# Crossbar transposes in layer norm and SwiGLU, and the earlier weight gradient stage

## The chip, the cores and the metric

The kernel runs on one core of a Trainium2 chip. The time is that of one execution on the device, in microseconds (us), as the median of repeated runs. TensorE (PE) multiplies matrices into PSUM, VectorE (DVE) and ScalarE (ACT) work elementwise and copy PSUM out, GpSimd (POOL) does small elementwise work, and SyncE (SP) issues transfers. ScalarE and GpSimd can issue transfers too. All transfers run on the core's 16 DMA engines. The "crossbar" below is the path in those engines that transposes two-byte data on its way.

## What is computed

Forward and backward of a block with layer norm, a segment-recurrent attention with memory, and a SwiGLU gate. There are S = 2048 rows of D = 640, H = 32 heads of 128, F = 1728, 64 segments of 32 rows, each with 8 memory rows. All tensors are bfloat16.

```python
xn = layernorm(x)                                  # rows, no affine part
mem = mem0                                         # 8 rows
for s in range(64):                                # one after the other
    h = concat([mem, xn[32*s:32*s+32]])            # 40 rows
    q, k, v = h @ Wq, h @ Wk, h @ Wv               # 32 heads of 128
    p = softmax(mask(q @ k.T * 128**-0.5))
    o = (p @ v) @ Wo
    mem, out_s = o[:8], o[8:]
z = (silu(xn @ w1) * (xn @ w3)) @ w2
out = x + concat(out_s) * silu(z)
# returned: out, and the gradients of x, mem0, Wq, Wk, Wv, Wo, w1, w3, w2
```

The stages in order are: layer norm; forward SwiGLU; the projections of the first rows; the forward chain over segments; the output stage; the backward chain; the weight gradients (with the part of x's gradient that comes through q, k and v); Wo's gradient; w2's gradient; the backward SwiGLU loop with layer norm's backward; the gradients of w1 and w3.

## The kernel before, where the change touches it

A transpose is made in one of two ways: on TensorE into PSUM, followed by a copy, or by the crossbar.

```python
def turned_load(k, dst, src):
    k.nc.sync.dma_start_transpose(dst, src)

# layer norm: xn is stored twice, as it is and turned
k.dma(k.XN[tt * P:(tt + 1) * P, :], xn[:])
for dc in range(DC):
    nc.tensor.transpose(pt[:, dc, :], xn[:, dc * P:(dc + 1) * P], k.ident[:])
k.copy(xnT[:], pt[:])
k.dma(k.XNT[...], xnT[:])

# forward SwiGLU, 4 blocks of 512 rows, 14 chunks of F (the last has 64 rows)
nc.gpsimd.dma_start(Wv[:], ...); k.x_rows(k.HRO, k.XN, nc.gpsimd)   # Wk follows at block 1
nc.scalar.dma_start(xnT[:], k.XNT[...])
for fc in range(FC):
    ...                                    # 5 matmuls into pg, 5 into pu, 128x512 each
    sig = sigmoid(pg); sl = pg * sig; ut = copy(pu); hBT[fc] = sl * ut
    ds = ...                               # three VectorE operations
    nc.sync.dma_start(k.SLT[...], sl); nc.sync.dma_start(k.DUT[...], ds)   # sl, ds: 2 buffers
for ti in range(BLK // P):
    ...                                    # 28 matmuls 128x320 into pz; gb, dz, gs; stores on nc.sync
    # 5 transposes of gs, copied, stored as GST; 14 transposes of hBT, copied in halves, stored as HB

# weight gradients: 8 groups of four heads (qd), 22 tiles of 120 rows (96 x rows, then 24 memory rows)
NF = NTL - 2; NB = 5; order = [NF, NF + 1] + list(range(NF))
def dturn(u):                              # dS turned by the crossbar
    turned_load(k, dST[:], st["l", u][0][:].rearrange("p j c -> p (j c)"))
def s2(u):                                 # gradients of v, k, q for one tile
    for i in range(3):                     # lhs = (P, dS, dST)
        ...                                # 4 matmuls into r6p (2 PSUM banks), copied to gr
        # the two last tiles are spilled to GSP and fill partitions 120 to 127 of gr
def s3(u):                                 # x rows only: 12 transposes 96x96 into t6g, copied to a ring
def s4(u):                                 # each full 128 x rows: 2 x 12 matmuls 128x320, added to acc
def wg(qd, i):                             # 20 tiles x 5 matmuls 128x512
for p in range(NTL):
    s2(u + 3); ld_to(u + 3 + NB); dturn(u + 4); s3(u + 2); s4(u)     # with bounds

# Wo's gradient: rows of OR on nc.sync, two buffers; hb loaded from HB on nc.scalar along the way
# w2's gradient: per row tile, 5 transposes of gz into one PSUM buffer, copied into gzT,
# which lies in one tile with w1T and w3T (crossbar loads); then 448 matmuls 128x320 (w2a)
# backward SwiGLU, 8 blocks of 256 rows
pg = ...                                   # 5 matmuls 128x256 per chunk; ggT = pg * du, guT = pg * sl
pgx = ...                                  # 56 matmuls 128x320 per row tile; PSUM: psC bufs=2, psD bufs=1
for (gT, dst) in ((ggT, ggtok), (guT, gut)):
    ...                                    # 14 transposes, copied by VectorE and ScalarE
nc.sync.dma_start(GU[rows, :], gut[:])
# w1, w3: 320 matmuls 128x432 with ggtok, then 320 with gutok_all, loaded from GU
```

Of the kernel before, what the change touches and what calls it, by code (L numbers as in the profile page):

```python
# [40 lines left out]
class K:  # L41
# [76 lines left out]
    def build_masks(self, pool, scr):  # L118
        nc = self.nc
        GE = ALU.is_ge  # L120
        n, nx = 120, 96
# [7 lines left out]
        for (c0, w) in ((nx, 8), (0, 32)):  # L129
            v1 = a1[:, c0:c0 + 3 * w].rearrange("p (s c) -> p s c", c=w)  # L130
            v2 = a2[:, c0:c0 + 3 * w].rearrange("p (s c) -> p s c", c=w)
            sel(v1, 1, -nx, [[-8, 3], [0, w]])
            sel(v1, -1, nx + 7, [[8, 3], [0, w]])
            sel(v2, 1, 0, [[-32, 3], [0 if w == 8 else -1, w]])
            sel(v2, -1, 31, [[32, 3], [0, w]])
# [8 lines left out]
        sel(b1[:], 1, -32, [[0, 40]])  # L144
        sel(b2[:, 0:32], 1, 0, [[-1, 32]])
# [6 lines left out]
    def setup_dram(self):  # L152
# [7 lines left out]
        self.XNT = mk("XNT", (D, S))  # L160
        self.SLT = mk("SLT", (F, S))
        self.DUT = mk("DUT", (F, S))
        self.HB = mk("HB", (S, F))
# [3 lines left out]
        self.GST = mk("GST", (D, S))  # L167

        self.NR = S + 8 * T
        self.GXA = mk("GXA", (S, D))  # L170
# [23 lines left out]
        for tl in range(self.NTL):  # L194
            n = self.geo(tl)[3]
            self.PR.append(mk(f"PR{tl}", (n, H, P)))
            self.DSR.append(mk(f"DSR{tl}", (n, H, P)))
# [3 lines left out]
        self.GSP = mk("GSP", (8, 3, 160, 512))  # L201
# [26 lines left out]
    def m_src(self, tl, w, c0, c1):  # L228
# [3 lines left out]
        r0 = self.geo(tl)[2]  # L232
        while t < end:
            e = min(end, t - t % 4 + 4)
            XS = self.store(w)[t // 4, g, 0:8, t % 4:t % 4 + e - t]
            for i in range(2 if w == "qv" else 1):
                X = XS[:, :, i] if w == "qv" else XS
                out.append((r0 + 8 * (t - 3 * tl), r0 + 8 * (e - 3 * tl), X[:, :, c0 - 1024 * g:c1 - 1024 * g].rearrange("r t c -> t r c"), i))
# [8 lines left out]
    def m_rows(self, A, t):  # L247
        r = 120 * (t // 3) + self.geo(t // 3)[2] + 8 * (t % 3)
        return A[r:r + 8, :]

    def x_rows(self, A, X, eng):
        n = self.NTL - 1
        eng.dma_start(A[0:120 * n, :].rearrange("(t r) d -> t r d", r=120)[:, 0:96],
                      X[0:96 * n, :].rearrange("(t r) d -> t r d", r=96))
        eng.dma_start(A[120 * n:120 * n + 32, :], X[96 * n:self.S, :])


# [102 lines left out]
def phase3_Afwd(k, W4, Wv, Wk_):  # L360
# [5 lines left out]
    with tc.tile_pool(name="b0", bufs=1) as io, tc.tile_pool(name="b0s", bufs=3) as stp, \  # L366
            tc.tile_pool(name="b0p", bufs=4, space=bass.MemoryType.PSUM) as ps:
        xs = io.tile([P, DC, k.NB0], BF16, name="b0x")
        nc.sync.dma_start(xs[:], k.XNT[:, 0:k.NB0].rearrange("(dc p) t -> p dc t", p=P))
# [21 lines left out]
    with tc.tile_pool(name="ast", bufs=1) as st, tc.tile_pool(name="achain", bufs=1) as ch, \  # L391
# [22 lines left out]
        def ride_ld(t):  # L414
            x0 = k.NB0 + 24 * t
            b, sub = t // 4, t % 4
            if sub == 0 and x0 < S:
                w = min(96, S - x0)
                rt = ch.tile([P, DC, 96], BF16, name="ride", tag="ride")
                nc.sync.dma_start(rt[:, :, 0:w], k.XNT[:, x0:x0 + w].rearrange("(dc p) s -> p dc s", p=P))  # L420
# [145 lines left out]
        def ld(w, tl, qd, eng=nc.sync):  # L566
# [4 lines left out]
            k.load_x(r, 0, k.x_src(tl, w, c0, c0 + 512), eng)  # L571
# [11 lines left out]
        def scores(tl, qd):  # L583
# [8 lines left out]
            for j in range(4):  # L592
                kv = kT[:, h0 + j, 0:n].rearrange("p (s c) -> p s c", c=40)
                nc.tensor.matmul(sp[:, j, nx:n], qT[:, j, :], kv[:, :, 0:8], start=False, stop=True,
                                 skip_group_check=True)
                nc.tensor.matmul(sp[:, j, 0:nx], qT[:, j, :], kv[:, :, 8:40], start=False, stop=True,
# [19 lines left out]
        def norm(tl, qd, eng=nc.gpsimd, q=nc.gpsimd):  # L616
# [6 lines left out]
            q.dma_start(k.PR[tl][:, h0:h0 + 4, :], Pb[0:n])  # L623
# [19 lines left out]
        def pv(tl, qd, q=nc.gpsimd):  # L643
# [3 lines left out]
            if 4 * tl < k.NO:  # L647
                pt = ps.tile([P, 4, 96], F32, name="xot", tag="x", bufs=5)
                for j in range(4):
                    nc.tensor.matmul(pt[:, j, :], v[0:n, j * P:(j + 1) * P], PTs[qd % 2][0:n, j, 0:96], start=True, stop=True)  # L650
# [110 lines left out]
def gx_ld(k, xs, x0, eng):  # L761
    w = min(P, k.S - x0)
    eng.dma_start(xs[:, :, 0:w], k.GST[:, x0:x0 + w].rearrange("(dc p) t -> p dc t", p=P))
# [13 lines left out]
def phase3b_out(k, Wo, W0, W4):  # L777
# [12 lines left out]
    with tc.tile_pool(name="oio", bufs=1) as io, tc.tile_pool(name="oac", bufs=1, space=bass.MemoryType.PSUM) as pa, \  # L790
# [6 lines left out]
        def ld(b, qd):  # L797
# [3 lines left out]
            if nt == 3:  # L801
                src = k.OR[120 * tl:120 * tl + 360, c0:c0 + 512].rearrange("(t r) c -> r t c", r=120)[0:96]
            else:
                src = k.OR[120 * tl:120 * tl + nx, c0:c0 + 512].rearrange("(t r) c -> r t c", t=1)
# [45 lines left out]
        def gox_ld(x0):  # L850
            xs = io.tile([P, DC, P], BF16, name="g0x", tag="g0x", bufs=2)
            gx_ld(k, xs, x0, nc.scalar)
# [34 lines left out]
        while g0:  # L887
# [6 lines left out]
    later = [(k.GWO[0:120 * n, :].rearrange("(t r) d -> t r d", r=120)[:, 0:96], k.GS[0:96 * n, :].rearrange("(t r) d -> t r d", r=96)),  # L894
             (k.GWO[120 * n:120 * n + 32, :], k.GS[96 * n:k.S, :])]

    for s in range(3):
# [3 lines left out]
        for b in range(2):  # L901
            dst = k.HRO[120 * tl0:120 * tl0 + 120 * (n - 1), :].rearrange("(t r) d -> t r d", r=120)[:, 96 + 8 * s:104 + 8 * s]
# [3 lines left out]
            later.append((k.m_rows(k.HRO, t1 + 1)[:, cols], k.FS[t1, 32 * b:32 * b + 8, :]))  # L906
# [998 lines left out]
```

## Time and profile before

| | before |
|---|---|
| median of 3 runs | 5610.01 us (5604.01 to 5610.44) |
| span of the profiled execution | 5608.7 us |
| granted TensorE clock, mean | 0.936 |
| TensorE matmul busy | 4787.0 us (85%) |
| TensorE weight loads busy | 3029.7 us (54%) |
| VectorE, ScalarE, GpSimd busy | 2245.6, 1758.4, 1562.8 us |
| moved by DMA | 845.92 MB in 1,100,096 packets, 602,753 of them under 512 B |
| forward chain (521 to 1841 us) | 1320 us, TensorE busy 1166.05 |
| output stage (1898 to 2020 us) | 122 us, DMA share 1.02 |
| backward chain (2147 to 3415 us) | 1268 us, TensorE busy 1163.37 |
| w1 and w3 gradients (5485 to 5609 us) | 124 us, TensorE busy 118.64 |

The busy time of an engine is the sum of its instructions. A group of instructions is one line of the kernel with one operation and shape; its idle time is what the engine stood still just before such instructions, with the releaser that came last. The clock is the share of full speed that TensorE was granted. The DMA share is the mean busy share of the 16 engines.

### The profile page before, as it was taken

What the parts mean: (1) busy time and instruction counts of PE and PEld (TensorE: products, weight loads), DVE (VectorE), ACT (ScalarE), POOL (GpSimd) and SP (SyncE); (2) the same over time, 40 slices, a digit from 0 to 9 for tenths busy, and PEclk for the clock granted to TensorE, in tenths of its full rate; (3) what the DMA queues carried; (4) which work ended last, traced back from release to release, by engine and by line L of the source; (5) the groups of instructions that cost most, each with busy time, mean ns of one, the idle gap of its engine ahead of it and who ended that gap; (6) DMA issues with size and microseconds to landing.
All of it is one profiled execution on the core that took longest, in us unless ns stands there. A gap on an engine that the chain in (4) does not pass through costs nothing. (4 is left out here: it accounts for less than half of the span.)

```text
span 5608.7 us, 161247 instructions
## 1 busy us (share of the span) xinstructions
PE 4787.0 (85%) x64913; PEld 3029.7 (54%) x65308; DVE 2245.6 (40%) x7110; ACT 1758.4 (31%) x4913; POOL 1562.8 (28%) x2675
## 2 busy tenths in 40 slices
PE   4987888888898767989899995978888888799999
PEld 2554555555555434656565663555455545566665
DVE  5833555555555323445454441232122212211451
ACT  2422555555555322323333321222122212200111
POOL 0000334434443122333333333234223423210000
PEclk9998999999999778999999997999999999899999
DMA  7553455555544696667666657576547655657332
GB/s 248 171 184 89 137 160 157 159 157 157 159 151 138 155 175 160 182 182 194 180 183 174 183 160 135 109 145 130 108 103 140 134 104 114 139 178 187 104 117 91
DMA packets 1100096, 845.92 MB, mean 151 GB/s; under 512 B 602753, under 2 KB 988077, under 8 KB 1096673
## 3 DMA queue, kind: packets, MB, share of 16 engines
q1 hardware_dynamic: 854523, 582.31, 40.0%
q0 software_dynamic: 95696, 155.10, 10.9%
q10 hardware_dynamic: 149130, 98.17, 6.4%
q8 instruction: 515, 8.44, 0.7%
q14 instruction: 232, 1.90, 0.1%
HBM read 476.95 MB, written 303.09 MB: 139 GB/s over the span
## 5 line engine op out<-in xcount | busy, mean ns | idle before, releaser
L1410 PE MATMUL wg<-gr,hr 128*128 128x512 bf16 x2352 | 532.6, 386 | 16.5 <-DVE grs L1353 7.6
L1389 PE MATMUL g<-w,ghacc 128*128 128x320 bf16 x3072 | 471.8, 314 | 0.0
L1410 PEld LDWEIGHTS <-hr 128*128 128x128 bf16 x2400 | 237.9, 99 | 305.0 <-issue 35.8
L1389 PEld LDWEIGHTS <-ghacc 128*128 128x128 bf16 x3072 | 309.8, 103 | 129.9
L308 PEld LDWEIGHTS <-hx 128*32 128x32 bf16 x7680 | 179.2, 97 | 168.0 <-issue 10.2
L1344 PE MATMUL r6p<-r,dST 120*128 120x128 bf16 (+1 forms) x704 | 74.7, 234 | 224.6 <-DMA dST<-dS 121.3
L90 DVE CAST wgo<-wg 128x512 bf16<-128x512 f32 x72 | 47.5, 688 | 539.0 <-PE wg L1410 289.5
L90 DVE CAST stg<-bank 128x512 bf16<-128x512 f32 x256 | 177.1, 692 | 206.5 <-PE bank L308 204.1
L327 PEld LDWEIGHTS <-gkv 128*8 128x8 bf16 x8192 | 190.5, 87 | 107.9 <-DVE gkv L1002 24.9
L611 ACT ACTIVATE xP<-xsp,xnm 120x120 bf16<-120x120 f32 (+1 forms) x704 | 240.5, 376 | 10.6 <-DVE xnm L607 5.2
L245 POOL DMA_DIRECT2D r<-GOS x256 | 144.0, 565 | 291.8 <-PE r6p L1344 221.8
L660 POOL DMA_DIRECT2D OR<-xv x163 | 93.0, 570 | 472.2 <-ACT xv L659 350.0
L1154 POOL DMA_DIRECT2D DSR<-gdS x176 | 101.5, 576 | 428.0 <-DVE gdS L1152 403.6
L92 ACT CAST wgo<-wg 128x512 bf16<-128x512 f32 x48 | 25.8, 589 | 595.8 <-PE wg L1410 595.8
L622 POOL TENSOR_TENSOR xP<-xP,xrz 120x480 bf16<-120x480 bf16 x163 | 161.9, 993 | 136.2 <-ACT xP L611 96.2
L1398 DVE TENSOR_TENSOR ghacc<-ghacc,g 128x320 f32<-128x320 f32 x192 | 93.7, 488 | 251.0 <-PE g L1389 251.0
L1344 PEld LDWEIGHTS <-dST 120*128 120x128 bf16 (+1 forms) x704 | 55.0, 103 | 247.4 <-DMA dST<-dS 151.1
L1351 ACT CAST gr<-r6p 120x512 bf16<-120x512 f32 x160 | 94.0, 588 | 295.1 <-PE r6p L1344 294.9
L1152 DVE SCALAR_TENSOR_TENSOR gdS<-gdp,Dx,gPr 120x120 bf16<-120x120 f32 (+1 forms) x680 | 182.9, 331 | 0.0
L1223 PE MATMUL gbank<-WqT,ident 128*128 128x512 bf16 x453 | 161.0, 405 | 20.7 <-issue 13.1
L308 PE MATMUL gbank<-WoT,gox 128*32 128x512 bf16 x2560 | 154.2, 387 | 25.2 <-POOL gox L957 21.9
L327 PE MATMUL bank<-Wo,oTm 128*32 128x320 bf16 x4032 | 171.9, 323 | 0.1
(339 smaller groups left out, 10933.5 us busy)
## 6 DMA issues: line engine op xcount, KB each, us to landing
QVS<-stg SPq DMA_DIRECT2D x128, 256.0 KB
gqv<-QVS SPq DMA_DIRECT2D x108, 192.0 KB
vTt<-VTD SPq DMA_DIRECT2D x64, 320.0 KB
VTD<-gvT POOLq DMA_DIRECT2D x168, 120.0 KB, 3.6
DSR<-gdS POOLq DMA_DIRECT2D x168, 120.0 KB, 3.6
dS<-DSR SPq DMA_DIRECT2D x168, 120.0 KB
P<-PR SPq DMA_DIRECT2D x168, 120.0 KB
gPr<-PR SPq DMA_DIRECT2D x164, 120.0 KB
```

The source lines that it names most:

```text
L90: return nc.vector.tensor_copy(out, in_)
L245: eng.dma_start(d, src if src.shape[0] > 1 else src[0])
L308: k.nc.tensor.matmul(bank[32 * g:32 * g + 32, :], x[:, dc, :], W[:, dc, c0:c0 + 512], start=(dc == 0), stop=(dc == k.DC - 1), tile_positio ...
L327: k.nc.tensor.matmul(pm[p0:p0 + nq, 0:320], x[:, h, :], W[:, h, 320 * b:320 * b + 320], start=(first and i == 0), stop=(last and i == 15), ...
L611: nc.scalar.activation(Pb[0:n, j, 0:n], sp[0:n, j, :], ACT.Exp, bias=nmx[0:n, j:j + 1], scale=k.scale, accum_out=Z[0:n, j:j + 1])
L622: eng.tensor_tensor(Pb[0:n, :, 0:n], Pb[0:n, :, 0:n], bc_last(rz[0:n], n), ALU.mult)
L1152: nc.vector.scalar_tensor_tensor(dS[0:n, j, 0:n], dp[0:n, j, :], Dx[0:n, j:j + 1], Pr[0:n, j, 0:n], op0=ALU.subtract, op1=ALU.mult)
L1154: nc.gpsimd.dma_start(k.DSR[tl][:, h0:h0 + 4, :], dS[0:n])
L1223: nc.tensor.matmul((bA if g in ("W1", "G1", "G2") else bB)[:], k.ident[:], WqT[:, 0, 0:512], start=True, stop=True)
L1344: nc.tensor.matmul(pr[:, j * P:(j + 1) * P], lhs[i][0:n, j, :], rw[i][0:n, j * P:(j + 1) * P], start=True, stop=True)
L1389: nc.tensor.matmul(pg[:], ring[:, i, j, r0:r0 + P], Ws[qd][i][:, j, 320 * h:320 * h + 320], start=(i == 0 and j == 0), stop=(i == 2 and j ...
L1410: nc.tensor.matmul(accs[dc][:], hr[:, tl, dc * P:(dc + 1) * P], grs[i][:, tl, :], start=(tl == 0), stop=(tl == NF - 1))
```

## The change

It has two parts. Layer norm and both SwiGLU stages let TensorE turn nothing any more: normalized rows, GS, h, gz and gg are turned by the crossbar, either from DRAM when they are loaded or from SBUF to SBUF, so that PSUM and the copies out of it are spared. As all crossbar transposes are issued by SyncE, the stores and plain loads of these stages go to GpSimd's and ScalarE's queues. In return, the weight gradient stage is the earlier one: it also takes the memory rows through the part that yields x's gradient (20 windows of 128 rows rather than 16), has 22 tiles of 120 rows in the weight products instead of 20 filled to 128, turns dS on TensorE instead of by the crossbar, and has three buffers for its loads instead of five. With it, the memory rows come first in each tile of 120 again, and P and dS are stored with rows of 120 instead of 128.

```diff
 # layer norm
-            for dc in range(DC):
-                nc.tensor.transpose(pt[:, dc, :], xn[:, dc * P:(dc + 1) * P], k.ident[:])
-            xnT = io.tile([P, DC, P], BF16, name="xnT_t", tag="xnT_t")
-            k.copy(xnT[:], pt[:])
-            k.dma(k.XNT[:, tt * P:(tt + 1) * P].rearrange("(dc p) t -> p dc t", p=P), xnT[:])
 # forward SwiGLU
-            nc.scalar.dma_start(xnT[:], k.XNT[:, b0:b0 + BLK].rearrange("(dc p) t -> p dc t", p=P))
+            turned_load(k, xnT[:], k.XN[blk * BLK:(blk + 1) * BLK, :])       # in fetch(), a block ahead
-                nc.sync.dma_start(k.SLT[fc * P:fc * P + fsz, b0:b0 + BLK], sl[:fsz])
-                nc.sync.dma_start(k.DUT[fc * P:fc * P + fsz, b0:b0 + BLK], ds[:fsz])
+                nc.gpsimd.dma_start(k.SLT[fc * P:fc * P + fsz, b0:b0 + BLK], sl[:fsz])
+                nc.gpsimd.dma_start(k.DUT[fc * P:fc * P + fsz, b0:b0 + BLK], ds[:fsz])
-                # transposes of gs and of hBT, their copies, stores of GST and of HB by rows
+            nc.gpsimd.dma_start(k.HB[0:(FC - 1) * P, b0:b0 + BLK].rearrange("(c p) t -> p c t", p=P), hBT[:, 0:FC - 1, :])
 # projections, rides of both chains, GS for the output stage (the same pattern)
-        nc.sync.dma_start(xs[:], k.XNT[:, 0:k.NB0].rearrange("(dc p) t -> p dc t", p=P))
+        turned_load(k, xs[:], k.XN[0:k.NB0, :])
 # weight gradients
-    NF = NTL - 2
-    NB = 5
+        NB = 3
-            dST = io.tile([P, 4, P], BF16, name="dST6", tag="dST6", bufs=4)
-            turned_load(k, dST[:], st["l", u][0][:].rearrange("p j c -> p (j c)"))
+            for j in range(4):
+                nc.tensor.transpose(pt[:, j, :], dS[0:n, j, :], k.ident[0:n, 0:n])
+            nc.vector.tensor_copy(dST[0:n, :, 0:n], pt[0:n])                 # s1(u), two buffers
-            nc.sync.dma_start(dS[0:n], k.DSR[tl][:, h0:h0 + 4, :])
-            nc.sync.dma_start(Pr[0:n], k.PR[tl][:, h0:h0 + 4, :])
+            nc.sync.dma_start(dS[0:n, :, 0:n], k.DSR[tl][:, h0:h0 + 4, :])
+            nc.sync.dma_start(Pr[0:n, :, 0:n], k.PR[tl][:, h0:h0 + 4, :])
+            for tl in range(NTL):
+                u = u0 + tl
+                ld(u + 4)
+                s2(u + 2, 0); s2(u + 2, 1); s1(u + 3); s3(u + 1, 0, 2); s2(u + 2, 2); s3(u + 1, 2, 3)
+                s4(u)                                                        # with bounds
 # Wo's gradient
-                nc.sync.dma_start(orrs[q][:, h * a:h * a + h, :], ...)
+                nc.scalar.dma_start(orrs[q][:, h * a:h * a + h, :], ...)
+        for f in range(0, F, 432):
+            late.append((hb[:, :, f:f + 432], k.HB[f:f + 432, :]))           # turned_load
 # w2's gradient and backward SwiGLU
-                        # 5 transposes of gz, copied
+                        turned_load(k, gzT[:, :, tt * P:(tt + 1) * P], gz[:, tt, :])
-                            # 14 transposes of ggT and 14 of guT, copied; GU stored by rows
+                                turned_load(k, ggtok[:, b0 // P:b0 // P + 2, fc * P:fc * P + fsz], ggT[0:fsz, fc, :])
+                        nc.gpsimd.dma_start(GU[0:FR, cols].rearrange("(c p) t -> p c t", p=P), guT[:, 0:FC - 1, :])
-                        tc.tile_pool(name="c5pc", bufs=2, space=bass.MemoryType.PSUM) as psC, \
-                        tc.tile_pool(name="c5pd", bufs=1, space=bass.MemoryType.PSUM) as psD:
+                        tc.tile_pool(name="c5pc", bufs=4, space=bass.MemoryType.PSUM) as psC, \
+                        tc.tile_pool(name="c5pd", bufs=2, space=bass.MemoryType.PSUM) as psD:
-                    nc.scalar.dma_start(gutok[:, t0:t0 + 2, :], GU[t0 * P:(t0 + 2) * P, :].rearrange("(t p) f -> p t f", p=P))
+                    turned_load(k, gutok[:, :, 432 * f:432 * f + 432], GU[432 * f:432 * f + 432, :])
```

The last load stands in `for f in range(4)`. GXA, which carries x's gradient through q, k and v to the last loop, has 2,560 rows instead of 2,048, and is read there in pieces of 32 to 96 rows.

## The prediction

> **What bounds the kernel now.** I first read the page's slices: TensorE is 80 to 99% busy nearly everywhere, so the time is TensorE's work plus its pauses, and a mean over the kernel says little. So I cut the span into stages and read busy times stage by stage. Columns: stretch, length, then busy us of TensorE, of its weight loads, VectorE, ScalarE, GpSimd, then granted clock, DMA share, GB/s.
>
> ```profile
> 0.00:62.00 62.00, 11.19 (x81) 7.57 (x82) 33.18 (x143) 11.30 (x25) 3.35 (x22) 1.00 0.82 255
> 62.00:330.00 268.00, 226.63 (x1293) 118.32 (x1310) 176.62 (x360) 99.85 (x161) 3.13 (x4) 0.92 0.55 186
> 3415.00:3460.00 45.00, 1.17 (x8) 0.79 (x9) 1.24 (x3) 0.54 (x1) 13.98 (x26) 0.54 0.91 176
> 3460.00:4960.00 1500.00, 1257.50 (x9640) 793.34 (x9687) 360.74 (x711) 356.78 (x576) 491.83 (x886) 0.92 0.60 122
> 4960.00:5137.00 177.00, 175.70 (x1280) 125.87 (x1280) 29.28 (x65) 12.03 (x32) 24.19 (x46) 0.99 0.74 232
> 5137.00:5225.00 88.00, 74.57 (x528) 48.05 (x528) 9.98 (x24) 9.59 (x21) 1.43 (x2) 0.92 0.47 93
> 5225.00:5485.00 260.00, 240.23 (x1904) 164.10 (x1905) 145.53 (x353) 42.78 (x65) 26.67 (x23) 0.99 0.38 117
> ```
>
> These are layer norm, forward SwiGLU, the start of the weight gradients, the weight gradients, the Wo gradient, the w2 gradient and the backward SwiGLU. The two recurrent chains (1,320 and 1,268 us) stand between them and are hardly touched. The weight gradients are the odd stage: 243 us of their 1,500 have no matmul, and the clock is 0.92. The groups and the timeline of that stage say why:
>
> ```profile
> L1344 PE MATMUL r6p<-r,dST 120*128 120x128 bf16 x672 | 71.3, 234 | 221.9 <-DMA dST<-dS 121.3 <-ACT gr L1351 69.0 <-ACT grs L1351 31.4
> ```
> ```profile
> 4043.26 3.42 PE L1389 MATMUL g<-w,ghacc 128*128 128x320 bf16 x24
> 4046.53 0.39 PE L1344 MATMUL r6p<-r,P 120*128 120x128 bf16 x4
> 4046.75 0.39 PE L1344 MATMUL r6p<-r,dS 120*128 120x128 bf16 x4
> 4051.11 0.60 PE L1344 MATMUL r6p<-r,dST 120*128 120x128 bf16 x4 [3.97 <-DMA dST<-dS]
> 4051.51 1.17 PE L1374 MATMUL t6g<-ident,gr 96*128 96x96 bf16 x12
> 4052.48 5.46 PE L1389 MATMUL g<-w,ghacc 128*128 128x320 bf16 x24
> ```
>
> The turned dS comes by crossbar and is late again and again; and after such a pause the same 24 matmuls take 5.46 us instead of 3.42. In an undisturbed unit TensorE still waits 0.45 us for ScalarE's copy before the third r6p group. Two more pauses lie in the chain that ended last (start, length, what):
>
> ```profile
> 5147.94 18.26 DMA x<-in_B_w_dram
> 5230.34 8.31 DMA sl<-SLT
> ```
>
> **What the skill says.** "DMA: Bandwidth & Descriptors", Latency and other measured facts, gives a DMA transpose 261 GB/s when its middle dimension isn't contiguous. The trace disagrees. While the w1 and w3 transposes ran (5140 to 5166 us), the DMA view reads:
>
> ```profile
> q1 hardware_dynamic: 16223, 4.38, 103.4%
> ```
>
> that is 1.034 x 16 engines x 26 us = 430 engine-us for 16,223 packets (4.38 MB), 26.5 ns for one of some 256 B, or about 155 GB/s on 16 engines. I use 26.5 ns. The same page, Specifications, puts the least transfer at full rate at 512 B; the trace agrees in kind: 186 B packets of ScalarE's queue took 15 ns in the forward chain (12 GB/s an engine), 1,054 B packets of SyncE's 54 ns (19.5 GB/s). Its section Queues, rings and completion order says that an engine takes turns between queues but drains one queue in order; the trace of before keeps stores and bulk loads on different queues there, so it doesn't show that case. "TensorE: Matmul & The Clock Gate", Why this matters for your kernels, says that an idle gap over about 3 us puts the array back to half its clock; the 5.46 against 3.42 us above agrees.
>
> **Weight gradients, by unit.** A unit is one 120-row tile for four heads; a group of four heads has 22 units, and there are 8 groups. Costs at full clock from start to start in the timeline: four r6p matmuls 0.22 us, twelve 96-wide transposes 0.51 (so I estimate 0.64 at 120 wide, 0.21 for four), 24 g matmuls 3.26, and 100 wg matmuls 21.75.
> - Before, a group: 22 x (0.67 + 0.51) + 16 x 3.26 + 300 x 0.2175 = 26 + 52 + 65 = 143 us; + 22 x 0.45 for ScalarE + about 8 of bank waits around wg = 161. Measured 1500/8 = 187.5. So some 26 us a group go to late dST and to the slow clock after it.
> - After, the memory rows are back in: 20 windows instead of 16, 22 tiles in wg instead of 20, 120-wide transposes, and four more transposes a unit for dS: 22 x (0.67 + 0.21 + 0.64) + 20 x 3.26 + 330 x 0.2175 = 33 + 65 + 72 = 170 us. The 0.45 us is filled, because dS's transposes and eight others stand between the second and third r6p group. With the same 8 us around wg: 178.
>
> So 27 us of work are added to each group, but the path loses the crossbar wait. 8 x 178 = 1,424 against 1,500: -76. The start (45 us, held by a 3 MB load of hr with small loads queued behind it) no longer needs a dST before its first work: about -10. VectorE gets a 0.40 us copy more per unit (the chain's 120x480 copies take 0.40) and still has some 2.5 us of work in 4.8; ScalarE some 2.2. Packets: the dS and P loads fall to 240 B pieces, 960 of them instead of 240 of 1 KB; at about 20 ns that is 1.2 us of 16 engines a unit instead of 0.75, but 512 transpose packets (0.85 us) go. DMA shouldn't bind. With three buffers instead of five I add 20 us of new waits. Stage: -66.
>
> **Layer norm and forward SwiGLU (0 to 330).** Removed from TensorE: 80 transposes in layer norm, 304 in SwiGLU (17.6 + 7.9 us busy), with ScalarE's and VectorE's copies (25 and 10 us). At full clock the rest is 560 x 0.217 + 448 x 0.136 = 182 us. VectorE's own chain is 56 x 2.63 (0.685 + 0.684 + 0.420 + 0.419 + 0.417) + 16 x 2.61 = 189 us, so VectorE becomes the bound. Before, TensorE's queue holds the layer norm transposes, so the first SwiGLU matmul stands at 61.9 us. Now it needs four normalized tiles and one crossbar load of 2,560 packets (4.2 us, plus issue and landing): about 42 us. Layer norm's 29 us on VectorE then lies partly beside it. Against this: the stores of sl and ds, two buffers each, now share GpSimd's queue with Wv, HRO and Wk (about 13 MB), so some 40 us of the early overlap stall. I put the end at 285 instead of 330: -45. Block 0 of the projections then waits for a 3,360-packet crossbar load (5.6 us) instead of a plain one: +4.
>
> **Output stage and chains.** The output stage has DMA at 1.02; four crossbar loads of GS come on top: +3. Rides by crossbar (14 in each chain, 0.8 us of DMA) and PR stores in 240 B pieces lie beside matmuls: 0.
>
> **Wo gradient and SwiGLU backward.** Wo gradient: hb comes by crossbar, 27,648 packets = 46 us of DMA instead of an estimated 19; 0.74 x 177 + 27 = 158 of 177 us, still hidden: 0. The w2 stage loses its 80 transposes (about 6 us) and the 18.26 us wait, since gzT's copy no longer stands in TensorE's way; 448 x 0.136 = 61 plus a little: 68 instead of 88, -20. In the block loop 448 transposes go: 14 take 1.0 us, so 32 us, and their copies (16 x (0.52 + 0.52) on VectorE, which feeds the accumulators), with twice the PSUM buffers: 560 x 0.114 + 896 x 0.151 = 199 plus load waits, 215 instead of 260: -45. The last stage: four crossbar loads of GU start only when the loop has ended, 46 us of DMA plus about 8 of drain, against 60 us of matmuls ahead of them: just hidden, +3 for risk. Sum -62.
>
> **Sum.** -66 - 45 + 4 + 3 - 62 = -166; 5610 - 166 = about 5,444. I shade it to 5,440.
>
> **Rivals.**
> - The added work shows and the waits stay: dS, P and row loads with three buffers are late as dST was. Then a group costs 170 + 8 + 26 = 204, the stage +132 over before, and the whole 5,640. For it: 60% DMA share already, small packets. Against it: the crossbar needed a load, a wait on SyncE and a transpose in series, the load alone only the first, with about two units (9.5 us) to land.
> - Stores behind bulk loads: the forward stage stalls until Wv, HRO and Wk are in, and gains nothing: about 5,490. For it: Wk took 41.5 us to land before. Against: those loads slowed the same stores before, from the other queue.
> - The crossbar becomes the bound in the backward stage (SyncE issues all transposes; gutok late): that stage gains only 30: about 5,470.
>
> **Range and chances.** The sum rests mostly on the weight gradients, where work and waits move against each other. If both smaller rivals come true in part, 5,520; if no new waits come and the loop runs clean, 5,360. Eight in ten: 5,350 to 5,560. Two per cent is 5,498 and below: 0.72; within 2%: 0.23; slower: 0.05.
>
> **What would show it.** Right: weight gradients near 1,440 to 1,450 us with TensorE busy over 93% and no wait on dS; first forward matmul near 42 us and VectorE over 90% busy after 110; backward loop near 215 with no gap at gutok. Wrong: TensorE waiting for dS, P or rows in the weight gradients; the clock there still 0.92; sl or ds waiting for SLT or DUT past 110 us.

## The result, and the profile after

The changed kernel takes 5,569 us (median of four runs, 5,551 to 5,573) against 5,610: a ratio of 0.992, interval 0.990 to 0.995. It is faster by 41 us where 170 were predicted, and lies outside the predicted 5,350 to 5,560. The same table of stages for the kernel after (columns as in the prediction: stretch, length, busy us of TensorE, its weight loads, VectorE, ScalarE, GpSimd, then granted clock, DMA share, GB/s):

```profile
39.00:300.00 261.00, 197.67 (x996) 96.56 (x1007) 179.79 (x405) 85.49 (x142) 96.83 (x172) 0.91 0.60 205
3409.00:3430.00 21.00, 1.92 (x14) 1.27 (x15) 1.15 (x3) 0.59 (x1) 11.09 (x21) 0.59 1.01 187
3430.00:4923.00 1493.00, 1409.62 (x11396) 915.07 (x11394) 457.14 (x989) 382.21 (x615) 453.80 (x818) 0.97 0.43 103
4923.00:5123.00 200.00, 183.66 (x1280) 128.31 (x1280) 29.26 (x65) 13.15 (x31) 24.01 (x46) 0.94 0.81 205
5123.00:5210.00 87.00, 66.27 (x448) 42.95 (x449) 7.17 (x18) 4.98 (x14) 2.97 (x5) 0.90 0.65 127
5210.00:5448.00 238.00, 211.77 (x1456) 138.55 (x1456) 125.55 (x315) 12.66 (x31) 47.34 (x52) 0.95 0.73 158
```

Side by side, from the same stretches and from the first and last matmul of each stage:

| stage | before | after | moved | predicted |
|---|---|---|---|---|
| start to the first projection matmul | 331.5 | 300.6 | -31 | -41 |
| forward chain (window) | 1,320 | 1,341 | +21 | 0 |
| start of the weight gradients | 45 | 21 | -24 | -10 |
| weight gradients | 1,500 | 1,493 | -7 | -56 |
| Wo gradient | 177 | 200 | +23 | 0 |
| w2 gradient | 88 | 87 | -1 | -20 |
| backward block loop | 260 | 238 | -22 | -45 |
| w1 and w3 gradients | 123 | 122 | -1 | +3 |

The rest (projections -4, prologue of the backward chain +8) is small. Three things stand out. TensorE is busier in the weight gradients (1,410 us instead of 1,258), at 0.97 of its clock instead of 0.92, in the same time: waits were exchanged for work. The Wo gradient, which was to stay hidden, has 16 us without a matmul and a clock of 0.94. And the w2 gradient lost its transposes (66 us busy instead of 75) but no time.

**Weight gradients, inside.** The timeline of TensorE in the middle of a group (start, duration, instruction):

```profile
4007.32 0.39 PE L1343 MATMUL r6p<-r,P 120*128 120x128 bf16 x4
...
4008.83 3.42 PE L1379 MATMUL g<-w,gT 128*128 128x320 bf16 x24
4012.09 0.39 PE L1343 MATMUL r6p<-r,P 120*128 120x128 bf16 x4
```

One unit takes 4.77 us from start to start, without a pause; the prediction's terms give 0.67 + 0.21 + 0.64 + 3.26 = 4.78. So the unit was priced right: 170 us a group, 1,363 in all. The other 130 us lie mostly at the heads of the groups. There the timeline of SyncE's queue (how long it took over each run of transfers) and that of TensorE read:

```profile
3966.66 29.50 SPq L1406 DMA_DIRECT2D out_dram<-wgo  x10
3996.25 0.39 SPq L1314 DMA_DIRECT2D dS<-DSR  x1
```
```profile
3995.85 0.38 PE L1343 MATMUL r6p<-r,P 120*128 120x128 bf16 x4 [1.95 <-DVE wgo L90]
...
3997.69 0.63 PE L1343 MATMUL r6p<-r,P 120*128 120x128 bf16 x4
...
3999.53 0.58 PE L1331 MATMUL t<-ident,dS 120*128 120x120 bf16 x4 [0.77 <-DMA dS<-DSR]
```

The dS of the fourth unit is written behind the ten last stores of wg in SyncE's queue, and these wait for wg to end. So it starts only when TensorE already wants it. Around it a group of four costs 0.58 to 0.63 us instead of 0.39: the granted clock is 1.00 until 3996 us and 0.57 from 3996 to 4004. The slow clock thus begins after the wait of 1.95 us for a copy of wg, ahead of the wait for dS. The groups view adds up the waits:

```profile
L1331 PE MATMUL t<-ident,dS 120*128 120x120 bf16 x700 | 68.9, 224 | 31.7 <-DMA dS<-DSR 28.2 <-DVE wgo L90 2.1 <-DVE gr L1348 0.7
```

Pauses are 1,493 - 1,410 = 83 us in all. 1,363 + 83 leaves 47 us. By the trace's record of the granted clock, 69 us of the matmul time ran at half clock, which costs some 35 us (an estimate: half of 69). The other 12 us are matmul time beyond the sum.

### The profile page after: what moved, and what is told of

The parts are those of the page before. It is cut to its first block, busy times and chain, and to the rows that moved or that the text cites. A ratio compares the mean times of both kernels' runs of the same rounds, so it can differ in the third digit from the quotient of the medians.

```text
span 5570.0 us, 163086 instructions
## 1 busy us (share of the span) xinstructions
PE 4878.7 (88%) x65768; PEld 3095.4 (56%) x66108; DVE 2311.4 (41%) x7334; ACT 1728.7 (31%) x4879; POOL 1685.9 (30%) x2802
## 5 line engine op out<-in xcount | busy, mean ns | idle before, releaser
L1401 PE MATMUL wg<-gr,hr 120*128 120x512 bf16 (+1 forms) x2640 | 587.9, 383 | 17.1 <-DVE dST L1333 13.0
L1379 PE MATMUL g<-w,gT 128*128 128x320 bf16 x3840 | 549.5, 300 | 0.0
L1401 PEld LDWEIGHTS <-hr 120*128 120x128 bf16 (+1 forms) x2640 | 257.8, 99 | 339.2 <-issue 45.4
L1379 PEld LDWEIGHTS <-gT 128*128 128x128 bf16 x3840 | 369.3, 98 | 137.0
L1388 DVE TENSOR_TENSOR ghacc<-ghacc,g 128x320 f32<-128x320 f32 x240 | 117.2, 488 | 276.4 <-PE g L1379 276.4
L1346 ACT CAST gr<-r6p 120x512 bf16<-120x512 f32 (+1 forms) x176 | 103.2, 587 | 362.9 <-PE r6p L1343 338.7
L92 ACT COPY gT<-t6g 128x960 bf16<-128x960 bf16 (+5 forms) x216 | 167.0, 792 | 121.5 <-PE t6g L1362 120.5
L1131 POOL DMA_DIRECT2D VTD<-gvT x176 | 130.7, 744 | 157.5 <-ACT gvT L1130 129.8
L1362 PE MATMUL t6g<-ident,gr 120*128 120x120 bf16 (+1 forms) x2112 | 172.5, 221 | 3.3 <-DVE wgo L90 2.7
```

The source lines that it names most:

```text
L92: return nc.scalar.copy(out, in_)
L1362: nc.tensor.transpose(pt[:, i - i0, j, :], st["g", u, i][0:n, j * P:(j + 1) * P], k.ident[0:n, 0:n])
L1379: nc.tensor.matmul(pg[:], ring[:, i, j, r0:r0 + P], Ws[qd][i][:, j, 320 * h:320 * h + 320], start=(i == 0 and j == 0), stop=(i == 2 and j ...
L1401: nc.tensor.matmul(accs[dc][:], hr[0:n, tl, dc * P:(dc + 1) * P], st["g", NTL * qd + tl, i][0:n, :], start=(tl == 0), stop=(tl == NTL - 1))
```

## Experiments: the weight gradients

**One more buffer for dS, P and rows.**

```diff
-        NB = 3
+        NB = 4
-                for i in range(3):      # loads ahead of wg's stores
+                for i in range(4):
```

> After the change, with four buffers instead of three for dS, P and rows in the weight gradients, so that the first four units of a group are loaded ahead of the stores of wg instead of three. Theory: dS of the fourth unit stands on SyncE's queue behind the stores of wg, so it comes late at the head of every group (28 us in all) and the array restarts at half clock (some 20 us more): the stage falls from 1,493 us to about 1,450, the whole to about 5,525. Rival: the pauses at the heads are accumulators waiting for copies, not loads; then the stage stays above 1,480 and the whole above 5,555.

Measured: 5,553 us, ratio 0.990 (0.988 to 0.992). The stage went from 1,491 to 1,470 us (first r6p of dST to last wg), the wait for dS from 28.2 to 12.8 us, of which 10.7 is the very first group, and the clock from 0.97 to 0.98. So both theories held in part. The queue cost some 21 us, which is more than the spread of this stage: it took 1,491 to 1,501 us in the nine kernels that leave it as it is. Of the 70 us of pauses that remain some 55 are waits for copies of accumulators, most of them around wg, and 53 us of matmul time still run at half clock.

**The kernel before, with dS turned by TensorE, between the second and third r6p group, and nothing else changed.** This separates the crossbar wait, which the change was to remove, from the memory rows, which it put back.

```diff
-            turned_load(k, dST[:], st["l", u][0][:].rearrange("p j c -> p (j c)"))
+            for j in range(4):
+                nc.tensor.transpose(pt[:, j, :], dS[0:n, j, :], k.ident[0:n, 0:n])
+            nc.vector.tensor_copy(dST[0:n, :, 0:n], pt[0:n])
```

> The kernel before, with one thing changed: dS turned by TensorE and VectorE instead of by the crossbar. Theory of the prediction (crossbar waits and half clock cost some 26 us a group): a group then has 22 x (0.67 + 0.21 + 0.51) + 16 x 3.26 + 65 = 148 us of work and, with the pauses that the changed kernel shows around wg (15 us), 163: stage about 1,305 instead of 1,500, whole about 5,415. Rival: the loads of dS and rows are themselves late, or SyncE's queue is blocked by stores as in the changed kernel; then the stage stays above 1,400 and the whole above 5,510.

Measured: 5,496 us, ratio 0.981 (0.977 to 0.985); the stage 1,401 us. It went past the changed kernel, but its stage stopped at the rival's figure, for a reason that neither theory had. TensorE's groups and ScalarE's timeline in that run:

```profile
L1352 PE MATMUL r6p<-r,dST 120*128 120x128 bf16 (+1 forms) x704 | 71.2, 226 | 110.0 <-ACT gr L1359 80.0 <-ACT grs L1359 25.2 <-DMA eo_s<-SR 2.8
```
```profile
4005.88 0.31 ACTq L267 DMA_DIRECT2D r<-GOS  x1
4006.29 0.80 ACT L92 COPY ghacc<-t6g 128x768 bf16<-128x768 bf16 x1 [4.28 <-DMA r<-QVS]
```

ScalarE issues the loads of gO's rows between its copies, in order. Its copy at 4006.29 came 4.28 us late because the load ahead of it could not go out yet, and TensorE waited for the copies behind.

**The same with those loads on SyncE.**

```diff
-                k.load_x(r, 0, src, nc.scalar if nm_ == "g" else nc.sync)
+                k.load_x(r, 0, src, nc.sync)
```

> The kernel before with dS turned by TensorE, as in the run before of that kind (stage 1,401 us), and the rows of gO in the weight gradients issued by SyncE instead of ScalarE. Theory: ScalarE is held up issuing those loads, so its copies of r6p and of the turned rows are late (105 us of TensorE waiting for ScalarE); the stage falls to about 1,310 and the whole to about 5,405. Rival: ScalarE's copies are late for want of buffers or accumulators; then the stage stays above 1,380, whole above 5,475.

Measured: 5,444 us, ratio 0.971 (0.968 to 0.973); the stage 1,357 us. The direction is the theory's, the size about half: 41.5 us of waits for ScalarE remain, 130 of them with at most 0.6 us, the 0.24 us in every unit before the third r6p group among them. The changed kernel has hardly any there (13, with 10.3 us in all), with eight transposes in between; that order is taken over in the last run below.

## Experiments: where the stages behind and ahead lost their gain

**The SwiGLU part alone.** The kernel before with the layer norm, SwiGLU and ride part of the change, but its own weight gradients, row order and 1 KB rows of P.

```diff
-        self.HB = mk("HB", (S, F))
+        self.HB = mk("HB", (F, S))
-                nc.sync.dma_start(rt[:, :, 0:w], k.XNT[:, x0:x0 + w]...)
+                turned_load(k, rt[:, :, 0:w], k.XN[x0:x0 + w, :])
+    # and layer norm, forward SwiGLU, Wo gradient, SwiGLU backward as in the kernel after
```

> The kernel before with only the layer norm and SwiGLU part of the change (crossbar loads, rides by crossbar, stores moved), its own weight gradients, row order and 1 KB rows of P. By the stages of the changed kernel: about -35 to the end of the projections, +8 ahead of the backward chain, +23 Wo gradient, -2 w2, -21 block loop, -2 last: about 5,580 if the forward chain keeps its old length (P stores are the cause of its 21 us), about 5,602 if the rides are.

Measured: 5,596 us, ratio 0.9986 (0.9974 to 0.9999). This half, priced at 100 us, gives almost nothing when alone, and the whole is nearer the figure for slow rides (5,602); the forward chain is taken up below. Its stages are those of the changed kernel: last forward matmul at 285, Wo gradient 195, w2 gradient 85, loop 232.

**GpSimd issues what ScalarE issued in the Wo and w2 gradients.**

```diff
-                nc.scalar.dma_start(orrs[q][...], ...)      # OR's columns
-                    nc.scalar.dma_start(out6f[...], ot[:])  # Wo's gradient
-                            nc.scalar.dma_start(out9[...], ot[...])  # w2's gradient
+    # the same three on nc.gpsimd
```

> After the change, with the stores of Wo's and w2's gradients and the loads of OR's columns put out by GpSimd instead of ScalarE. Theory: ScalarE, which also copies half of the accumulators, stands still while such a transfer waits for its turn behind crossbar loads; freed of them, the Wo gradient falls from 200 us to about 182 and the w2 gradient from 86 to about 71: whole about 5,536. Rival: the crossbar loads fill the DMA engines there (share 1.18) and nothing else can land whoever issues it; then Wo stays at 195 or more and w2 at 83 or more, whole about 5,565.

Measured: 5,553 us, ratio 0.990 (0.987 to 0.992). The w2 gradient fell to 71 us, the Wo gradient rose to 214 (32 us of waiting for OR's columns): the theory held for one and the rival for the other. Freeing ScalarE is not what the Wo gradient lacks.

**h's crossbar loads in twelve pieces; six buffers for sl and du; w2's stores on GpSimd.**

```diff
-        for f in range(0, F, 432):
-            late.append((hb[:, :, f:f + 432], k.HB[f:f + 432, :]))
+        for f in range(0, F, 144):
+            late.append((hb[:, :, f:f + 144], k.HB[f:f + 144, :]))
-                            sl = bp.tile(..., tag="sl5", bufs=3)   # and du5
+                            sl = bp.tile(..., tag="sl5", bufs=6)
```

> After the change, three edits in three stages behind the weight gradients. Wo gradient: h's crossbar loads in twelve pieces over tiles 4 to 11 instead of four pieces over tiles 4 to 7. Theory: the stage lost 23 us because these loads bunch (DMA share 1.18 for some 80 us, so OR's columns land late), not because of their sum; it falls from 200 us to about 182. Rival: crossbar loads and plain loads hinder each other however they are spread: 195 or more. w2 gradient: its stores on GpSimd's queue as in the run before of that kind, about 71 us. Block loop: six buffers instead of three for sl and du; if their loads start too late for want of buffers, 238 us falls to about 222; if ScalarE issues them late, it stays within 4 us. Whole about 5,520.

Measured: 5,565 us, ratio 0.993 (0.990 to 0.995). The block loop fell from 238 to 213 us. VectorE's waits in the changed kernel had been

```profile
DVE ggT L1740 <- DMA du<-DUT: 25.3, 16, 6.8
```

and this group is gone: three buffers started these loads too late. The Wo gradient stayed at 199: SyncE had nothing else in its queue, and put all twelve out in 56 us. So this run did not test spreading. The w2 gradient stayed at 83: ScalarE now had twelve prefetches of sl and du ahead of its copies. The whole did not follow. In the profiled execution the way from the end of the forward chain to the weight gradients, which it does not touch, was 18 us longer than in the profile of the changed kernel; whether that holds for the other executions is not shown. Stages are therefore read here, and wholes only by their intervals.

**Pieces that wait for the tiles, and VectorE's copies in the w2 gradient.** Before the change, SyncE's queue held Wo's stores.

```diff
-                    nc.scalar.dma_start(out6f[...], ot[:])
+                    nc.sync.dma_start(out6f[...], ot[:])
+    # twelve pieces of h and four of w2 between these stores, one or two a tile
-                            k.copy(ot[...], accs[i][...], eng='vs'[i % 2])
+                            k.copy(ot[...], accs[i][...], eng='v')
```

> After the change, with the stores of Wo's gradient put out by SyncE again, and h's and w2's crossbar loads in sixteen pieces between them in the written order, so that each piece waits for the tiles before it. The run with twelve pieces left the stage at 199 us, but SyncE put all twelve out in 56 us, one after the other, so it spread nothing. Theory (bunching): DMA share stays below 1 and the Wo gradient falls from 200 us to about 182. Rival (crossbar and plain loads hinder each other however spread): 195 or more. In the w2 gradient VectorE alone copies the accumulators, the stores staying with ScalarE. Theory: ScalarE's copies stand behind transfers that it cannot put out yet; the stage falls from 86 us to about 72. Rival: the stage waits for the crossbar loads of w1 and w3 themselves: 83 or more. Whole about 5,540.

Measured: 5,540 us, ratio 0.988 (0.985 to 0.992). Wo gradient 175 us, w2 gradient 69. In the changed kernel SyncE's timeline had the four pieces in one row, and from their middle on (length and columns as above) the DMA engines were full and TensorE was short of OR's columns:

```profile
4932.53 54.56 SPq L278 DMA_TRANSPOSE hb_all<-HB  x4
```
```profile
4963.00:5003.00 40.00, 32.38 (x205) 21.39 (x203) 3.71 (x8) 1.70 (x4) 3.19 (x6) 0.87 1.19 246
```

In this run, SyncE's timeline and two stretches:

```profile
4992.15 0.81 SPq L1550 DMA_DIRECT2D out_dram<-wgoo  x2
4993.01 4.68 SPq L278 DMA_TRANSPOSE hb_all<-HB  x1
```
```profile
4975.00:5015.00 40.00, 40.00 (x297) 28.78 (x295) 7.00 (x16) 3.01 (x8) 4.88 (x10) 1.00 0.84 225
5015.00:5055.00 40.00, 40.00 (x296) 28.79 (x295) 5.46 (x13) 2.36 (x6) 6.26 (x12) 1.00 1.13 275
```

A store, which waits for its tile, stands ahead of each piece, and TensorE doesn't pause, though the DMA share passes 1 once here too. This run also takes Wo's stores from ScalarE; but where ScalarE was freed of them and of the loads, the stage rose to 214 us. This points to the pace; a run with Wo's stores alone moved back was not made. In the kernel before, h's plain loads had stood between ScalarE's copies, one every 10.9 us:

```profile
5027.60 0.43 ACT L1550 CAST wgoo<-oa 128x320 bf16<-128x320 f32 x1 [10.11 <-PE oa L1544]
5027.90 0.37 ACTq L1537 DMA_DIRECT2D hb_all<-HB  x1
```

The change put them into SyncE's queue, and Wo's stores out of it, so that nothing in that queue waited for a tile any more. In the w2 gradient, ScalarE's timeline in the changed kernel shows what held the accumulators:

```profile
5140.95 0.76 ACT L92 CAST w2o<-w2a 128x320 bf16<-128x320 f32 x2 [16.95 <-DMA du<-DUT]
5150.18 9.27 ACTq L1712 DMA_DIRECT2D out_dram<-w2o  x5
5159.48 0.43 ACT L92 CAST w2o<-w2a 128x320 bf16<-128x320 f32 x1 [17.78 <-DMA x<-gz_all]
```

Five stores stood between two copies and took 9.3 us to put out, while crossbar loads from SyncE's queue held 91% of the DMA engines (5141 to 5160 us); TensorE waited 15.6 us for the second copy. With VectorE's copies these stores are as late as before, but nobody waits for them.

**Stores of sl and ds on SyncE again.**

```diff
-                nc.gpsimd.dma_start(k.SLT[...], sl[:fsz])   # and DUT
+                nc.sync.dma_start(k.SLT[...], sl[:fsz])
```

> After the change, with the stores of sl and ds in the forward SwiGLU put out by SyncE again instead of GpSimd. Theory: on GpSimd's queue they stand behind the loads of Wv, HRO and Wk, which stops the stage for 27 us from 68 us on; the last forward matmul then moves from 284 us to about 262 and the whole to about 5,548. Rival: the bulk loads take the DMA engines (about 300 GB/s there) from the stores whatever queue they are on; then the last forward matmul stays at 278 us or later, whole about 5,565.

Measured: 5,564 us, ratio 0.992 (0.990 to 0.994); last forward matmul at 283 us. Both are the rival's figures. In the changed kernel TensorE's timeline shows one long stall,

```profile
102.04 0.59 PE L1626 MATMUL pu<-xnT_b,w3s 128*128 128x512 bf16 x1 [27.49 <-ACT ut L1633]
```

here there are two, of 9.2 and 11.9 us, again with VectorE waiting for a store of ds (8.5 and 13.4 us), and from 150 to 200 us TensorE is busy for 41 us instead of 48. From 72 to 102 us GpSimd's queue, with the bulk loads, has 57% of the DMA engines and SyncE's 10%. So the bulk loads delay these stores from another queue as well. Later stalls could also come from the next block's crossbar load, which now shares SyncE's queue with the stores; this run does not separate them.

**Bulk loads in pieces of 1 MB; the crossbar load ahead of the projections in six.**

```diff
-        nc.gpsimd.dma_start(Wv[:], ...); k.x_rows(k.HRO, k.XN, nc.gpsimd)
+                if blk > 0 and fc % 3 == 1 and bulk:
+                    bulk.pop(0)()               # Wv, Wk by 1 MB, then HRO
-        turned_load(k, xs[:], k.XN[0:k.NB0, :])
+        for i in range(0, k.NB0, 112):
+            turned_load(k, xs[:, :, i:i + 112], k.XN[i:i + 112, :])
```

> After the change, two edits ahead of the forward chain. The loads of Wv and Wk go in five pieces of 1 MB each, put out one every three chunks from the second block on, HRO last, instead of 8 MB at once in the first block. Theory (bulk loads take the DMA engines from the stores of sl and ds, whatever queue): the stall of 27 us between 65 and 105 us goes and the last forward matmul moves from 284 us to about 258. Rival: VectorE's work limits the stage by then; 275 or later. And the crossbar load ahead of the projections goes in six pieces of 112 rows: the wait of 16.3 us falls to about 7. Whole about 5,535.

Measured: 5,552 us, ratio 0.991 (0.988 to 0.994). The last forward matmul came at 277 us instead of 284. That is the rival's figure, but not its reason: VectorE still waits 38.5 us for stores of ds, in 15 pieces of up to 12 us. What would end these waits stays open: pieces of 256 KB with four buffers for sl and ds (the last run) gave 275. The second edit did what it should: 7.9 us from the last forward matmul to the projections instead of 16.3.

## Experiments: the forward chain

The profile of the changed kernel has a chain 20 us longer, though its computation there is the same. GpSimd's groups in the forward chain, before and after:

```profile
L623 POOL DMA_DIRECT2D PR<-xP x161 | 91.6, 569 | 50.7 <-POOL xP L622 41.3 <-DVE xrz L621 6.2 <-issue 3.2
```
```profile
L629 POOL DMA_DIRECT2D PR<-xP x161 | 136.8, 850 | 59.5 <-POOL xP L628 35.5 <-DVE fsum L345 11.9 <-issue 7.1
```

GpSimd needs 0.85 us to put out one store of P in 240 B pieces, 0.57 in 1 KB pieces. What a late P leads to stands in TensorE's timeline of the changed kernel:

```profile
1156.54 0.18 PE L361 MATMUL bank<-sel,fsum 64*128 64x8 bf16 x1 [0.82 <-DVE fsum L345]
...
1158.59 0.38 PE L636 MATMUL xpp<-ident,xP 120*128 120x120 bf16 x4 [0.83 <-POOL xP L628]
...
1159.29 3.95 PE L314 MATMUL bank<-Wk,hx 128*32 128x512 bf16 x40
```

The same 40 matmuls take 2.34 us in the next step. So I held the stores of P for the cause, and the rides by crossbar for the rival.

```diff
-            self.PR.append(mk(f"PR{tl}", (n, H, n)))      # and DSR
+            self.PR.append(mk(f"PR{tl}", (n, H, P)))
-            q.dma_start(k.PR[tl][:, h0:h0 + 4, :], Pb[0:n, :, 0:n])
+            q.dma_start(k.PR[tl][:, h0:h0 + 4, :], Pb[0:n])
```

> After the change, with the rows of P and dS in memory 128 wide again (1 KB pieces for four heads instead of 240 B each). Theory: in the forward chain GpSimd takes 0.85 us instead of 0.57 to put out one store of P in 240 B pieces; three in a row make the third product late, TensorE pauses and restarts at half clock. Then the chain falls from 1,341 us in the window to about 1,320 and the whole to about 5,548. Rival: the rides by crossbar slow the chain; then this run is at 5,569 and the chain unchanged.

```diff
-                turned_load(k, rt[:, :, 0:w], k.XN[x0:x0 + w, :])
+                nc.sync.dma_start(rt[:, :, 0:w], k.w1[:, c:c + w].rearrange("(dc p) s -> p dc s", p=P))
```

> After the change, with the 14 rides of the forward chain loaded plainly (of w1's columns in place of the turned rows, so the values are not the reference's; pieces and bytes as before the change). Rival: if the crossbar loads slow the chain, it gets its 20 us back, about 5,549. Theory (stores of P): within 3 us of 5,569, the steps of the chain as uneven as before.

Measured: 5,553 us, ratio 0.991 (0.988 to 0.994), with wide rows of P; 5,566 us, ratio 0.992 (0.990 to 0.995), with plain rides, whose data are w1's columns instead of the turned rows. The chain, from the first turn of Pm to the last, was 1,313.5 and 1,307.1 us, against 1,321.3 after and 1,301.1 before: in these profiles both moved it, the rides more. So the dose was raised:

```diff
                 turned_load(k, rt[:, :, 0:w], k.XN[x0:x0 + w, :])
+                turned_load(k, r2[:, :, 0:w], k.XN[x0:x0 + w, :])   # a spare tile
```

> After the change, with each of the 14 rides of the forward chain loaded a second time by crossbar into a spare tile. In the profiles so far the forward chain (first to last turn of Pm) is 1,301 to 1,303 us in the three kernels with plain rides and wide P, 1,307 with plain rides and narrow P, 1,309 to 1,320 with crossbar rides and wide P, 1,314 to 1,321 with both. If the crossbar rides lengthen the chain by some 12 us, twice as many should make it about 1,330; if the differences are the P stores and the chance of half-clock steps, it stays within 1,314 to 1,321.

Measured: 5,572 us, ratio 0.994 (0.992 to 0.996), chain 1,305.9 us: shorter. So the crossbar rides are not the cause; nor is the whole without them (5,566 us) clear of the changed kernel's. Taking for each of the 63 steps the shortest that any profile shows, a chain would be 1,278 us; every profile has between 14 (before) and 26 (after) steps that take 0.6 to 4.0 us more, and they are mostly other steps each time. The record of the granted clock shows what most of them are. In the step shown above, during its 40 matmuls, it stands at 0.50 (columns as in the stages' table):

```profile
1161.00:1163.20 2.20, 2.20 (x25) 0.58 (x18) 0.69 (x1) 0.00 (x0) 1.38 (x2) 0.50 0.57 110
```

Such half clock comes in stretches of 3.4 us, sometimes two together: 18 of them in the chain before, 27 after. All 14 slow steps before and 22 of the 26 after touch one. Profiles with 17 or 18 stretches have chains of 1,301 to 1,307 us, those with 24 to 29 chains of 1,313 to 1,321. So most of the 20 us is half clock. Late P is a small part: inside the chain TensorE waits for it 3.6 to 5.1 us with narrow rows in all profiles but one, which has no such wait, and 0 to 2.1 us with wide rows. Nor does it bring the half clock: that one profile has 25 stretches, and the joined kernel of the next part, with wide rows and no wait for P in the chain, 29. Why half clock is more frequent after the change is open. Narrow rows with crossbar rides gave 1,314 to 1,321 us seven times and 1,306 with the rides doubled; wide rows with plain rides gave 1,301 to 1,303 three times and 1,310 once.

## Experiments: both parts joined

The kernel before with dS turned by TensorE and gO's loads on SyncE, the SwiGLU part, and the edits of the two runs with twelve pieces and with 1 MB pieces:

> The kernel before with dS turned by TensorE and gO's rows issued by SyncE in the weight gradients (the run of that kind: stage 1,357 us), its own row order and 1 KB rows of P, together with the layer norm and SwiGLU part of the change and the edits of the two runs beside this one. From 5,444: -13 for the SwiGLU part as measured alone, -15 for the Wo gradient, -15 for w2, -10 for the loop, -30 ahead of the chain: about 5,360. If the edits get in each other's way, 5,420 or more.

Measured: 5,397 us, ratio 0.964 (0.962 to 0.967), between the two figures expected. The chain took 1,320 us here, with wide rows of P, and the Wo gradient 203.

The same with the pieces that wait for tiles, VectorE's copies for w2, plain rides from a turned copy of xn that is stored from the crossbar's result, bulk loads of 256 KB, four buffers for sl and ds, and in the weight gradients:

```diff
-                    s2(u + 3, lambda: dturn(u + 4))
+                    s2(u + 3, lambda: (dturn(u + 4), s3(u + 2, ((0, 2),))))
```

> The joined kernel again (its weight gradients 1,357 us, whole 5,397), with the rides and the projections' block loaded plainly from a turned copy that is stored from the crossbar's result (chain 1,320 to about 1,304, wait ahead of the projections about 8 us); sixteen paced pieces for h and w2 and VectorE's copies as in the run beside this one (Wo 203 to 182, w2 77 to 72); in the weight gradients eight turns between the second and third r6p group, so that ScalarE's copy is no longer waited for (130 waits of 0.3 us: -35); Wv and Wk in pieces of 256 KB, one a chunk, and four buffers for sl and ds (last forward matmul from 275 us to about 262). Sum: about 5,310; 5,360 or more if the weight gradients do not give.

Measured: 5,344 us, ratio 0.954 (0.950 to 0.957), the fastest of all. Its stages, weight gradients first, then Wo, w2 and the loop:

```profile
3423.00:4756.00 1333.00, 1231.66 (x10336) 803.54 (x10383) 412.33 (x884) 348.44 (x576) 489.31 (x883) 0.97 0.51 123
4759.00:4933.00 174.00, 173.63 (x1279) 125.11 (x1280) 27.95 (x63) 11.47 (x30) 23.20 (x44) 1.00 0.93 235
4934.00:5005.00 71.00, 66.48 (x448) 42.54 (x449) 10.33 (x25) 0.00 (x0) 1.43 (x2) 0.98 0.79 163
5006.00:5216.00 210.00, 202.81 (x1455) 136.64 (x1454) 123.37 (x316) 12.44 (x30) 47.73 (x52) 0.98 0.82 176
```

The weight gradients gave 24 us of the 35 expected; waits for ScalarE's copies of gr fell from 135 (43.4 us) to 35 (24.0 us). The head gave nothing new: last forward matmul at 275 us, and 14.3 us to the projections instead of 8. The chain was 1,310.

## Why the prediction was wrong, step by step

- **Weight gradients, -66.** "8 x 178 = 1,424": the work in it, 170 us a group, was right to 0.01 us a unit. The mis-sized term is what lies around wg: 8 us a group plus 20 in all, 84 us, for pauses. The pauses alone were 83 us; but behind them the clock is half, and that term, which the same prediction saw in the kernel before (5.46 for 3.42 us), is missing from the sum for after: some 35 us. The other 12 us are matmul time beyond the sum. The start gave 24 us instead of 10. The sign "TensorE busy over 93%" came true (1,410 of 1,493 us is 94%), but matmuls at half clock count as busy too.
- The deeper point: "27 us of work are added to each group, but the path loses the crossbar wait" set 26 us of wait against 27 of work, and took the gain from a hidden ScalarE wait and smaller terms. Turning dS by TensorE without the memory rows shows the two apart: 1,500 to 1,333 us, 21 us a group, for the wait with its half clock and ScalarE's part; and 1,333 against 1,470 with the memory rows and four buffers, 17 us a group. The first rival (loads with three buffers late) came true for some 21 us of the 1,493, not as the waits in the middle of a group that it described.
- **Wo gradient, 0.** "158 of 177 us, still hidden" averaged the DMA engines' load over the stage. The loads were not spread: SyncE put them out in 55 us, and the share was 1.20 there. What failed is the average; spread, the stage takes 175 us.
- **w2 gradient, -20.** The work is right (69 us once ScalarE is out of the way, 68 predicted). Not priced was that the moved stores stand between ScalarE's copies: 15.6 us of TensorE's waiting.
- **Block loop, -45.** "199 plus load waits, 215" is right in its work and wrong in the waits, which made it 238; with six buffers in place of three it took 213.
- **Layer norm and forward SwiGLU, -45.** First matmul at 39 us (42 predicted), last at 284 (285). The end is right in part by luck, for the bound is not VectorE: from 150 to 250 us it is 85% busy and TensorE 97%. The stall of "some 40 us" was 27, for which GpSimd's queue was blamed; on SyncE's queue it stayed, so the shared engines cause it, or both. The wait for the projections' block grew by 9 us, not 4: SyncE took 13.4 us to put out that one transfer.
- **Chains, 0.** Wrong by 20 us for the forward chain in the profile. "Beside matmuls" holds for the rides, shown by doubling them. Most of the 20 us is half clock, in 27 stretches instead of 18; waits for P with its narrow rows are some 4 us. What brings the half clock stays open.
- **Last stage, +3.** Right within 4 us: gutok's crossbar loads stayed hidden, though their 46 us rest on the same reading of 26.5 ns.
- The rival "the crossbar becomes the bound in the backward stage" gave the stages behind the weight gradients a gain of 30 instead of 62. Together they gained 1. Its form (gutok late) did not show; what the crossbar loads cost was their bunching in the Wo gradient and the stores that stood still beside them in the w2 gradient.

One reading of the trace was wrong too: the cost of a crossbar packet was put too high. 26.5 ns is a mean over 26 us in which other loads ran and some slices were nearly empty. Where the crossbar loads of w1 and w3 have the engines nearly to themselves, the kernel before shows (columns as in the stages' table)

```profile
5143.10:5147.00 3.90, 3.90 (x39) 2.82 (x37) 0.77 (x2) 1.39 (x2) 0.00 (x0) 1.00 1.26 287
```

287 GB/s instead of 155, or some 14 ns for 256 B on one of 16 engines. So the trace shows no less than the 261 GB/s of the Trainium skill ("DMA: Bandwidth & Descriptors", Latency and other measured facts), and h's 27,648 packets alone are some 25 us of DMA instead of 46 (an estimate from the 287 GB/s). The sum for the Wo gradient was too cautious, and the stage still lost 23 us, which again points to the bunching.

## What to carry to other kernels

A wait is best removed without buying it with work of the same size: ask what else would remove it, and price that first. When stores or loads change queues, ask what each queue's order did: which transfers it paced, and which engine's own work now stands behind a transfer that cannot start. A DMA share averaged over a stage says nothing of the 50 us in which all its loads start.

## What the runs showed of the hardware that was not expected

- GpSimd's time to put out a store grows with the number of its pieces: 0.57 us for P in 120 pieces of 1 KB, 0.85 us for the same rows in 480 pieces of 240 B.
- Pauses far shorter than 3 us are followed by half clock: 0.82, 0.49 and 0.83 us within 3 us, then 40 matmuls in 3.95 us instead of 2.34. The Trainium skill, "TensorE: Matmul & The Clock Gate", Why this matters for your kernels, speaks of an idle gap over about 3 us; here several short ones were enough, in some steps and not in others. The granted clock was 0.50 in stretches of 3.4 us.
- One crossbar load of 3,360 packets held SyncE for 13.4 us (13.4 to 16.5 us in the ten kernels that have it), beside plain loads of the projections' weights; in six pieces each took 1.2 to 3.9 us.
- Crossbar loads of 256 B packets moved 287 GB/s from 5143.1 to 5147 us of the kernel before.
